# Fused attention and two expert layers on one core: q tiles loaded ahead, half of the pack products moved into the first unit, another scratch order

## The chip, the cores and the metric

One core of a Trainium2 chip (trn2). The metric is the device time of one execution in microseconds, lower is better. The engines are TensorE (PE; its weight loads are PEld), VectorE (DVE), ScalarE (ACT), GpSimd (POOL) and SyncE (SP), whose queue issues nearly all transfers of the kernel before.

## The reference, cut to what matters

```python
def _attn_ref(q, k, v, p):                  # q, k, v: 8 x 8 x 576 x 64; p: 8 x 8 x 32 x 64
    p_packed = sm_attn(p, k, v)             # 32 packs per head attend to 576 keys
    return sm_attn(q, p_packed, p_packed)   # 576 queries attend to the 32 packs
# x = that, as 4608 tokens x 512
h = np.maximum(x @ w_in, 0.0)               # 512 x 2048
x = h * h @ w_out                           # 2048 x 512
# then one of 8 experts (512 -> 1024 -> 512) for each token, by the argmax of its gate
```

`sm_attn` is a softmax attention with scale 1/8. The inputs are float32, but `w_in` and `w_out` arrive as float64.

## The kernel before, in words

The output of the second attention is never built. For each batch the packed heads are multiplied with `w_in` once, head by head: pw has 256 rows (8 heads x 32 packs) and 2048 columns for a batch, and the softmax weights of the second attention (256 for a token) times pw are the hidden layer.

**Opening.** `with tc.manual_schedule()` (L901) writes the order out by hand. A loop over i = 0 .. 18 (L914) runs a pipeline over 16 quads (a batch and half of its heads): `scores(i)` on PE, `greatest` and `normalise` on VectorE and ScalarE, `turn_a(i - 2)` and `values(i - 3)` on PE, and `packs(i - 3)` (L356), which copies the packed heads into `pp33`. Beside it `load_k`, `load_v` and `load_in` issue transfers on SyncE, a slab of `w_in` is converted from float64 (`conv_in`, four VectorE operations and one on ScalarE), and from i = 10 a step of `att2(0)` (L429) is taken: the second attention of the first 384 tokens, in three tiles of 128, of three steps each. A tile's first step issues the load of its q tile (L436, tile `qT`, two buffers) and then the scores against `pp33` (L440). So the loads of the three q tiles are issued at i = 10, 13 and 16.

From i = 11 `pw_quad` (L366), called a pack product here, is taken: for four batches, a pair of heads and a block of 512 columns two 64-row products on PE (j = 0, 1), a copy from PSUM into a staging tile `pws` (L388 on ScalarE or L390 on VectorE, two buffers), and a store of 512 KB on SyncE to the scratch `pw_d` (L391). There are 16 for batches 0 to 3 and 16 for 4 to 7. Five are in i = 11 .. 15, then two, three and four, then ten in a loop (L958) among four `conv_out` (the slabs of `w_out`) and the first `split_pw`; the last eight come in the first unit, in `others` (L975), where the two copies are one on each engine (L385, L386). `load_pw` (L406) brings a block of pw back (batch, 512 columns) in four transfers of 128 KB; it needs the four stores of that block. `split_pw` (L413) cuts it into two parts of reduced precision on ScalarE and GpSimd.

**Main loop.** Twelve units of 384 tokens (L1017); for each of 16 row blocks f of the hidden layer `layer1` (L475) multiplies pw with the softmax weights (L486, or L492 to L495 where a unit lies in two batches), squares, and `layer2` (L508) accumulates with `w_out` (L512). `att2` of the next unit, the gate of the unit before and the routing run beside it. The two expert layers follow (L802, L824).

Every engine, SyncE too, takes its instructions in the program's order; behind the opening a scheduler in the framework sets that order when the kernel is built, and may put the first unit's instructions between those of the opening's end. Eight slots count the transfers in flight: each transfer waits, on the engine that issues it, for the one eight places before it in the program.

## Time and profile before

| what | value |
|---|---|
| three runs, median (lowest to highest) | 1317.05 us (1314.45 to 1319.13) |
| the profiled execution | 1315.94 us, span 1314.0 us |
| PE busy | 1227.0 us, 93% of the span |
| DVE, ACT, POOL busy | 62%, 47%, 21% |
| mean granted TensorE clock | 0.967 |
| the chain that ended last | PE 69%, DVE 13%, DMA 10% |

Times in the profile are microseconds from the span's start. A busy share is an average over the stages, so the stages are read one by one.

### The profile page before, as it was taken

The page shows a single profiled execution, that of the slowest core. Times are in us where ns is not written, and L with a number is a line of the kernel's source. Part 1 is how long each engine was busy: PE and PEld are TensorE (multiplying, and loading weights), DVE is VectorE, ACT ScalarE, POOL GpSimd, SP SyncE. Part 2 cuts the span into 40 slices and gives each one's busy share as a digit, 9 for nine tenths or more (in the row PEclk, how much of TensorE's full clock was granted, in tenths as well). Part 3 has the DMA queues.
Part 4 walks back from the last instruction along what each step waited for, and adds up shares of the span by engine and source line. Part 5 has one row for each costly group of instructions (what it writes and reads, how often), then busy time and mean ns, then how long its engine had stood idle before and what let it go on. Part 6 is the DMA issues. An engine that isn't in the chain of part 4 may idle for free.

```text
span 1314.0 us, 17851 instructions
## 1 busy us (share of the span) xinstructions
PE 1227.0 (93%) x6036; PEld 989.3 (75%) x6036; DVE 815.0 (62%) x2141; ACT 617.4 (47%) x1292; POOL 281.4 (21%) x353
## 2 busy tenths in 40 slices
PE   7578579999999999999999999989999999999995
PEld 5455146888888888888888887877788888888884
DVE  7546477396874976569587578877843543354341
ACT  5334444667545665546755466641432432343230
POOL 4000444433200222102221023100320220132011
PEclk9879669999999999999999999999999999999998
DMA  9956876122201222102220112231532542453310
GB/s 349 352 195 202 271 234 214 57 73 57 66 17 44 83 63 65 33 25 65 75 72 25 49 33 85 88 137 57 194 107 86 194 145 84 159 176 104 106 65 34
DMA packets 76853, 149.22 MB, mean 114 GB/s; under 512 B 7248, under 2 KB 26832, under 8 KB 76624
## 3 DMA queue, kind: packets, MB, share of 16 engines
q1 hardware_dynamic: 70992, 128.81, 29.6%
q0 software_dynamic: 5760, 19.17, 4.6%
q8 instruction: 49, 0.80, 0.3%
q14 instruction: 52, 0.43, 0.1%
HBM read 112.01 MB, written 35.95 MB: 113 GB/s over the span
## 4 chain that ended last, share of the span: by engine, by line
PE 69%; DVE 13%; DMA 10%; issue 3%; ACT 2%; POOL 1%; SPq 1%; POOLq 0%; DVEq 0%; ACTq 0%
PE acc L512 22%; PE h L802 15%; PE o L824 15%; PE ph L486 9%; DVE rows L533 5%; DMA pw_d<-pws 3%; PE s L440 2%; DMA wraw<-in_moe_w 1%; DMA rows<-in_k 1%; DMA qT<-in_q 1%; DVE r L499 1%; DMA wgb<-in_k 1%; DVE ghl L505 1%; PE tr L782 1%; PE pq L354 1%
## 5 line engine op out<-in xcount | busy, mean ns | idle before, releaser
L512 PE MATMUL acc<-wb,ghl 128*128 128x512 f32 x1728 | 444.8, 400 | 3.8 <-ACT ghl L503 3.6
L512 PEld LDWEIGHTS acc<-wb,ghl 128*128 128x128 f32 x1728 | 319.7, 189 | 71.7 <-ACT ghl L503 8.9
L533 DVE SCALAR_TENSOR_TENSOR rows<-rows,wgb 128x512 f32<-128x512 f32 x288 | 213.4, 741 | 3.7
L802 PE MATMUL h<-xt,wb 128*128 128x512 f32 x864 | 214.9, 399 | 0.7 <-DVE ht L813 0.7
L802 PEld LDWEIGHTS h<-xt,wb 128*128 128x128 f32 x864 | 162.8, 189 | 40.6 <-DVE ht L813 1.7
L505 DVE TENSOR_TENSOR ghl<-r,ghl 128x384 fp32r<-128x384 f32 x176 | 103.7, 590 | 80.4 <-ACT ghl L503 80.0
L503 ACT ACTIVATE ghl<-r 128x384 fp32r<-128x384 f32 x192 | 100.2, 522 | 101.2 <-PE acc L512 99.3
L813 DVE SCALAR_TENSOR_TENSOR ht<-h,ht 128x512 fp32r<-128x512 f32 x72 | 49.2, 688 | 115.9 <-ACT ht L812 115.7
L824 PE MATMUL o<-head,ht 128*128 128x512 f32 x432 | 113.3, 396 | 3.8 <-ACT ht L812 3.4
L824 PE MATMUL o<-ring,ht 128*128 128x512 f32 x432 | 112.5, 395 | 0.0
L812 ACT ACTIVATE ht<-h 128x512 fp32r<-128x512 f32 x72 | 42.5, 593 | 144.8 <-PE h L802 144.7
L835 POOL DMA_INDIRECT out<-wgb,idx_s x36 | 36.7, 1019 | 344.8 <-DVE wgb L833 254.0
L502 ACT ACTIVATE r<-r 128x384 f32<-128x384 f32 x192 | 100.2, 523 | 4.6
L824 PEld LDWEIGHTS o<-head,ht 128*128 128x128 f32 x432 | 80.1, 188 | 23.3 <-ACT ht L812 4.5
L417 POOL TENSOR_TENSOR ring<-praw,ring 128x256 fp32r<-128x256 f32 x70 | 59.2, 850 | 177.9 <-ACT ring L416 169.7
L824 PEld LDWEIGHTS o<-ring,ht 128*128 128x128 f32 x432 | 80.1, 188 | 16.8
L486 PE MATMUL ph<-a2T,ring 128*128 128x384 f32 x420 | 86.0, 341 | 0.0
L501 ACT ACTIVATE r<-ph 128x384 f32<-128x384 f32 x128 | 61.6, 482 | 44.7 <-PE ph L486 36.6
L486 PEld LDWEIGHTS ph<-a2T,ring 128*128 128x128 f32 x420 | 74.3, 188 | 5.0 <-issue 0.9
L417 POOL TENSOR_TENSOR head<-praw,head 128x256 fp32r<-128x256 f32 x58 | 48.6, 841 | 133.8 <-ACT head L416 123.8
L460 POOL TENSOR_TENSOR e<-e,sm 128x256 f32<-128x256 f32 x36 | 27.2, 757 | 228.3 <-DVE sm L459 188.8
L486 PE MATMUL ph<-a2T,head 128*128 128x384 f32 x348 | 74.4, 347 | 1.8 <-DVE pws L390 1.4
(198 smaller groups left out, 1707.8 us busy)
## 6 DMA issues: line engine op xcount, KB each, us to landing
wraw<-in_moe_w SPq DMA_DIRECT2D x72, 512.0 KB, 3.8
pw_d<-pws SPq DMA_DIRECT2D x32, 512.0 KB, 4.1
praw<-pw_d SPq DMA_DIRECT2D x128, 128.0 KB, 2.9
x_d<-rows SPq DMA_DIRECT2D x12, 792.0 KB, 3.9
qT<-in_q SPq DMA_DIRECT2D x36, 256.0 KB, 2.9
early<-in_v SPq DMA_DIRECT2D x16, 512.0 KB, 8.9
stage<-in_moe_w_in SPq DMA_DIRECT2D x16, 512.0 KB, 8.9
rows<-in_k SPq DMA_DIRECT2D x10, 576.0 KB, 8.6
```

The source lines that it names most:

```text
L417: nc.gpsimd.tensor_tensor(out=t[:, 1], in0=raw, in1=t[:, 0].bitcast(F32), op=ALU.subtract)
L486: nc.tensor.matmul(ph, t[:, x, c, :], a[:, y, c, :], start=(i == 0), stop=(i == 3 * NPC - 1))
L501: nc.scalar.activation(out=r, in_=ph if len(ps) == 1 else r, func=AF.Relu)
L502: nc.scalar.activation(out=r, in_=r, func=AF.Square)
L503: nc.scalar.activation(out=hl[:, 0], in_=r, func=AF.Copy)
L505: eng.tensor_tensor(out=hl[:, 1], in0=r, in1=hl[:, 0].bitcast(F32), op=ALU.subtract)
L512: nc.tensor.matmul(acc[t], hl[:, x, t * P : (t + 1) * P], w_out_block(f)[:, y, :], start=(f == 0 and x == 0 and y == 0), stop=(f == NF - 1 ...
L533: nc.vector.scalar_tensor_tensor(out=junk, in0=row[:, t, :DM], scalar=1.0, in1=wgb[:, e], op0=ALU.mult, op1=ALU.mult, accum_out=one)
L802: nc.tensor.matmul(ph, half1(g, c)[:, x, f * P : (f + 1) * P], xs[c][:, y, :], start=(i == 0), stop=(i == 3 * NDC - 1),)
L812: nc.scalar.activation(out=h[:, 0, :], in_=ph, func=AF.Relu)
L813: nc.vector.scalar_tensor_tensor(out=h[:, 1, :], in0=ph, scalar=0.0, in1=h[:, 0, :].bitcast(F32), op0=ALU.max, op1=ALU.subtract)
L824: nc.tensor.matmul(po, hs[f][:, x, t * P : (t + 1) * P], second(f)[:, y, :], start=(i == 0), stop=(i == 3 * NFE - 1),)
```

## The change

1. The q tiles of the first unit: the first two are loaded at i = 6 and 7, the third behind the first tile's scores (`load_q`, `qts`).
2. `packs` writes the packed heads twice: `pp32`, with zeros beside them, for the scores of the second attention, now with the 64 columns side by side where they were four apart, and `ppq`, without zeros, for the pack products. The second is a copy on ScalarE.
3. Three, four and four pack products in i = 16, 17 and 18, none behind; the other 16 in the first unit, one at an even f and two at an odd one. Three staging tiles for two. Two of the four `conv_out` behind the loop move into the first unit.
4. Stores of products that ScalarE copies are issued by ScalarE; those of VectorE, and all of the first unit, by SyncE.
5. The scratch is ordered by batch, pack and head, so a block of pw comes back in one transfer of 512 KB. Its rows now go by pack and head, so the softmax tile `e` is stored that way and its operations go over it with a step of eight words.
6. To make room: one square tile for two, and the third raw tile of `w_out` is a part of `rows`.

```diff
-    pp33 = pp_p.tile([P, HP, B // 4, 2 * NPK, 4], F32, name="pp32")
+    pp32 = pp_p.tile([P, B, HP, 2 * NPK], F32, name="pp32")
+    ppq = pw_p.tile([P, HP, B, NPK], F32, name="ppq")
-    squares = [pw_p.tile([P, 512], F32, tag="sq", name="sq", bufs=2) for _ in range(2)]
+    squares = [pw_p.tile([P, 512], F32, tag="sq", name="sq") for _ in range(1)]
...
-    pw_d = tc.dram_tile([B // 4, H, P, DFF], F32, name="pw_d")
+    pw_d = tc.dram_tile([B, NPK, H, DFF], F32, name="pw_d")
...
-    RAWS_OUT = [wgf[:, :1024], wgf[:, 1024:2048], xraw]
+    RAWS_OUT = [wgf[:, :1024], wgf[:, 1024:2048], rows[:, :1024]]
...
         for j in range(2):
-            nc.vector.tensor_copy(
-                pp33[j * D : (j + 1) * D, 2 * qd : 2 * qd + 2, b // 4, j * NPK : (j + 1) * NPK, b % 4],
-                pq[j * D : (j + 1) * D, : 2 * own].rearrange("p (g x) -> p g x", g=2)[:, :, j * NPK : (j + 1) * NPK],
-            )
+            js, ns, gs = slice(j * D, (j + 1) * D), slice(j * NPK, (j + 1) * NPK), slice(2 * qd, 2 * qd + 2)
+            src = pq[js, : 2 * own].rearrange("p (g x) -> p g x", g=2)[:, :, ns]
+            nc.vector.tensor_copy(pp32[js, b, gs, ns], src)
+            nc.scalar.activation(out=ppq[js, gs, b, :], in_=src, func=AF.Copy)
...
-                pp33[js, hp, bq, j * NPK : (j + 1) * NPK].rearrange("p n b -> p (n b)"),
+                ppq[js, hp, 4 * bq : 4 * bq + 4].rearrange("p b n -> p (b n)"),
...
-        so = pw_p.tile([P, 2, 512], F32, tag="w5", name="pws", bufs=2)
+        so = pw_p.tile([P, 2, 512], F32, tag="w5", name="pws", bufs=3)
...
-        nc.sync.dma_start(
-            pw_d[bq].rearrange("(g j) r f -> g r j f", j=2)[hp][:, :, fb * 512 : (fb + 1) * 512], so
-        )
+        (nc.scalar if eng == "ACT" else nc.sync).dma_start(dst, so)
...
-        src = pw_d[b // 4].rearrange("(c h) r f -> h r c f", c=NPC)
-        for h in range(H // NPC):
-            nc.sync.dma_start(raw[h * NPK : (h + 1) * NPK], src[h, b % 4 :: 4, :, fb * 512 : (fb + 1) * 512])
+        nc.sync.dma_start(raw, pw_d[b].rearrange("(c n) h f -> (n h) c f", c=NPC)[:, :, fb * 512 : (fb + 1) * 512])
...
+    def load_q(t0):
+        qT = held["at"].tile([P, HP, P], F32, tag="qT", name="qT", bufs=2)
+        nc.sync.dma_start(qT, qT_d[:, t0 : t0 + P].rearrange("(g p) t -> p g t", p=P))
+        return qT
...
+            qT = load_q(t0) if t0 not in qts else qts.pop(t0)
...
-                        pp33[:, g, b // 4, :, b % 4],
+                        pp32[:, b, g, :],
...
+            if u == 0 and r + 2 < UT:
+                qts[t0 + 2 * P] = load_q(t0 + 2 * P)
...
-            e = held["at"].tile([P, H, NPK], F32, tag="e", name="e", bufs=1)
+            et = held["at"].tile([P, NPK, H], F32, tag="e", name="e", bufs=1)
+            e = et.rearrange("p n h -> p h n")
...
-            ef = e.rearrange("p h n -> p (h n)")
+            ef = et.rearrange("p n h -> p (n h)")
...
+            if i in (6, 7):
+                qts[(i - 6) * P] = load_q((i - 6) * P)
             if i >= 10:
                 next(bg)
-            for _ in range({16: 2, 17: 3, 18: 4}.get(i, 1 if i >= 11 else 0)):
+            for _ in range({16: 3, 17: 4, 18: 4}.get(i, 1 if i >= 11 else 0)):
                 pw_quad(0, made, "ACT" if i < 16 or made % 2 else "DVE")
...
-        for w in range(10):
-            bq, pu = divmod(made, NU)
-            pw_quad(bq, pu, "ACT" if made % 2 else "DVE")
-            made += 1
-            if w % 3 == 0:
-                for _ in conv_out(2 + w // 3):
-                    pass
-            if w in (2, 4, 6):
-                split_pw(0, w // 2)
+        for w in (2, 3):
+            split_pw(0, w - 1)
+            for _ in conv_out(w):
+                pass
+        split_pw(0, 3)
...
-        if made < 2 * NU:
-            pw_quad(1, made - NU, None)
-            made += 1
-        if f + 6 < NU:
-            for _ in conv_out(f + 6):
+        for _ in range(1 + f % 2):
+            if made < 2 * NU:
+                pw_quad(1, made - NU, None)
+                made += 1
+        if f + 4 < NU:
+            for _ in conv_out(f + 4):
```

The order that this gives on the engines, at three places. SyncE, the first q tile, before (the rows are i = 9's last transfers, the tile, and the next k tile behind it; `rows` and `wgb` hold k tiles, `stage` slabs of `w_in`, `early` v tiles):

```order
L242 DMA stage<-in_moe_w_in 128x1024
L281 DMA early<-in_v 128x1024
L284 DMA early<-in_v 64x256
L436 DMA qT<-in_q 128x4x128
L272 DMA rows<-in_k 128x2x576
```

And with the change, from i = 6 on:

```order
L281 DMA early<-in_v 128x1024
L284 DMA early<-in_v 64x256
L431 DMA qT<-in_q 128x4x128
L272 DMA rows<-in_k 128x2x576
L242 DMA stage<-in_moe_w_in 128x1024
L281 DMA early<-in_v 128x1024
L284 DMA early<-in_v 64x256
L431 DMA qT<-in_q 128x4x128
L272 DMA rows<-in_k 128x2x576
```

The tile moves ahead of four k tiles, their slabs and their v tiles; a second one follows an iteration later.

SyncE again, at the end of the opening, where blocks of pw are stored (from `pws`) and brought back (to `praw`, the first of these block 0 of batch 0, then block 1, then 2). Before:

```order
L391 DMA pw_d_135<-pws_902 128x2x512
L391 DMA pw_d_135<-pws_908 128x2x512
L410 DMA praw_911<-pw_d_135 32x2x512 x4
L391 DMA pw_d_135<-pws_952 128x2x512
L391 DMA pw_d_135<-pws_958 128x2x512
L391 DMA pw_d_135<-pws_964 128x2x512
L410 DMA praw_967<-pw_d_135 32x2x512 x4
L246 DMA wgb_84<-in_moe_w_out 128x1024
L391 DMA pw_d_135<-pws_1003 128x2x512
L391 DMA pw_d_135<-pws_1009 128x2x512
L410 DMA praw_1142<-pw_d_135 32x2x512 x2
L391 DMA pw_d_135<-pws_1015 128x2x512
```

With the change (`pws_935` is product 6, 984 and 996 are 8 and 10, 1040 and 1052 are 12 and 14, all counted from 0):

```order
L431 DMA qT_1390<-in_q 128x4x128
L393 DMA pw_d_134<-pws_935 128x2x512
L408 DMA praw_944<-pw_d_134 128x2x512
L393 DMA pw_d_134<-pws_984 128x2x512
L393 DMA pw_d_134<-pws_996 128x2x512
L408 DMA praw_1005<-pw_d_134 128x2x512
L246 DMA wgb_84<-in_moe_w_out 128x1024
L408 DMA praw_1102<-pw_d_134 128x2x512
L393 DMA pw_d_134<-pws_1040 128x2x512
L393 DMA pw_d_134<-pws_1052 128x2x512
```

The odd products' stores are gone from this queue, and block 2 is now asked for before the stores of products 12 and 14.

PE, inside the first unit (`pw` pack products, `ph` layer 1, `acc` layer 2), before:

```order
L512 MATMUL acc<-wb_1043,ghl 128x512 x3
L376 MATMUL pw<-wi_116,pp_85 128x512
L486 MATMUL ph<-a2T,head 128x384 x2
L376 MATMUL pw<-wi_116,pp_85 128x512
L486 MATMUL ph<-a2T,head 128x384 x6
L512 MATMUL acc<-wb_1100,ghl 128x512 x9
L376 MATMUL pw<-wi_116,pp_85 128x512 x2
```

And with the change:

```order
L493 MATMUL ph<-a2T,head 128x384 x8
L519 MATMUL acc<-wb_1076,ghl 128x512 x7
L376 MATMUL pw<-wi_113,ppq 128x512
L519 MATMUL acc<-wb_1076,ghl 128x512 x2
L474 MATMUL ta_1294<-ident,e 128x128 x2
L376 MATMUL pw<-wi_113,ppq 128x512
L493 MATMUL ph<-a2T,head 128x384 x9
L519 MATMUL acc<-wb_1130,ghl 128x512 x9
L376 MATMUL pw<-wi_113,ppq 128x512
L519 MATMUL acc<-wb_1130,ghl 128x512 x4
L376 MATMUL pw<-wi_113,ppq 128x512 x2
```

A row without a count is one 64-row product alone; `x2` is two that follow each other. The whole first unit holds ten alone and three pairs before, and 21 alone, four pairs and a run of three with the change.

## Rows read from the trace of the kernel before

**Rows 1.** The page's busy tenths in 40 slices, PE and its clock

```profile
PE   7578579999999999999999999989999999999995
PEclk9879669999999999999999999999999999999998
```

**Rows 2.** Windows: stretch, length, busy PE, PEld, DVE, ACT, POOL; clock, DMA share, GB/s

```profile
0.00:54.00 54.00, 41.30 (x293) 30.42 (x293) 40.76 (x104) 28.58 (x53) 17.97 (x47) 1.00 0.99 359
54.00:104.00 50.00, 30.49 (x173) 20.92 (x175) 19.66 (x52) 15.11 (x27) 2.32 (x3) 0.73 0.63 216
104.00:174.10 70.10, 44.89 (x191) 21.00 (x190) 37.48 (x64) 27.36 (x51) 21.52 (x25) 0.74 0.77 250
174.10:258.10 84.00, 80.30 (x336) 56.69 (x337) 47.73 (x77) 45.29 (x95) 37.68 (x33) 0.94 0.47 156
258.10:1314.00 1055.90, 1030.04 (x5047) 860.27 (x5046) 669.38 (x1846) 501.04 (x1068) 201.88 (x245) 0.99 0.26 84
```

**Rows 3.** Timeline of PE, 54 to 115 us: start, length, instructions, idle time before

```profile
66.02 1.94 PE L440 MATMUL s<-pp,qT 128*128 128x64 f32 x8 [13.72 <-DMA qT<-in_q]
...
82.51 2.50 PE L354 MATMUL pq<-atbuf,early 128*128 128x128 f32 x20
...
92.50 1.94 PE L440 MATMUL s<-pp,qT 128*128 128x64 f32 x8 [7.49 <-DMA qT<-in_q]
...
103.94 1.19 PE L307 MATMUL s<-wgb,ptb 128*64 128x288 f32 x8
...
114.78 1.15 PE L440 MATMUL s<-pp,qT 128*128 128x64 f32 x8 [3.02 <-DMA qT<-in_q]
```

**Rows 4.** Timeline of SyncE's queue (SPq), the first q tile's issue

```profile
57.66 0.39 SPq L436 DMA_DIRECT2D qT<-in_q  x1
```

**Rows 5.** Groups by line: count, busy us, mean ns, idle before: the copies

```profile
L388 ACT ACTIVATE pws<-pw 128x1024 f32<-128x1024 f32 x15 | 15.3, 1018 | 37.4 <-PE pw L376 19.2 <-DMA pw_d<-pws 16.1 <-issue 2.2
...
L390 DVE COPY pws<-pw 128x1024 f32<-128x1024 f32 x9 | 11.0, 1221 | 18.4 <-DMA pw_d<-pws 14.2 <-PE pw L376 4.2
...
L361 DVE COPY pp<-pq 64x64 f32<-64x64 f32 x32 | 8.7, 272 | 5.6 <-PE pq L354 5.2
```

**Rows 6.** Timeline of PE, 174 to 258 us, the first unit

```profile
174.12 2.29 PE L486 MATMUL ph<-a2T,head 128*128 128x384 f32 x6 [1.37 <-DVE pws L390]
...
196.50 1.12 PE L376 MATMUL pw<-wi,pp 64*128 64x512 f32 x2
...
219.51 1.13 PE L376 MATMUL pw<-wi,pp 64*128 64x512 f32 x4
...
220.56 2.35 PE L512 MATMUL acc<-wb,ghl 128*128 128x512 f32 x9
...
255.98 2.35 PE L512 MATMUL acc<-wb,ghl 128*128 128x512 f32 x9
```

**Rows 7.** Page, DMA issues: engine, count, size, us to landing

```profile
pw_d<-pws SPq DMA_DIRECT2D x32, 512.0 KB, 4.1
```

**Rows 8.** Waits, 104 to 174.1 us: total, times, longest

```profile
PE pw L376 <- ACT pws L388: 15.7, 8, 4.6
...
DVE pws L390 <- DMA pw_d<-pws: 14.2, 3, 7.0
```

**Rows 9.** Windows of 20 us, inside the first unit

```profile
200.00:220.00 20.00, 19.48 (x83) 12.19 (x83) 19.72 (x28) 11.55 (x23) 10.01 (x9) 1.00 0.46 153
```

**Rows 10.** Groups by line: the softmax of the second attention

```profile
L451 DVE TENSOR_TENSOR e<-s,mx 128x256 f32<-128x256 f32 x36 | 15.1, 419 | 1.5
...
L457 DVE TENSOR_REDUCE sm<-e 128x8 f32<-128x256 f32 x36 | 14.9, 414 | 5.4 <-ACT e L455 5.1
...
L455 ACT ACTIVATE e<-e 128x256 f32<-128x256 f32 x36 | 14.8, 410 | 10.4 <-DVE e L451 10.2
...
L460 POOL TENSOR_TENSOR e<-e,sm 128x256 f32<-128x256 f32 x36 | 27.2, 757 | 228.3 <-DVE sm L459 188.8 <-PE tb L339 25.9 <-DMA qT<-in_q 5.1
```

**Rows 11.** Waits of PE, 174.1 to 258.1 us

```profile
PE pw L376 <- ACT pws L385: 1.6, 1, 1.6
```

More of the change, by code (lines that the diff above doesn't have):

```diff
@@ L93, in tile_pack_attention_moe_moe2 @@
     wgb = wg_p.tile([P, NE, DM], F32, name="wgb")
-    pp33 = pp_p.tile([P, HP, B // 4, 2 * NPK, 4], F32, name="pp32")
-    nc.gpsimd.memset(pp33, 0.0)
-    squares = [pw_p.tile([P, 512], F32, tag="sq", name="sq", bufs=2) for _ in range(2)]
+    pp32 = pp_p.tile([P, B, HP, 2 * NPK], F32, name="pp32")
+    nc.gpsimd.memset(pp32, 0.0)
+    ppq = pw_p.tile([P, HP, B, NPK], F32, name="ppq")
+    squares = [pw_p.tile([P, 512], F32, tag="sq", name="sq") for _ in range(1)]
     whole = [pw_p.tile([P, 512], F32, tag="tf", name="tf", bufs=2) for _ in range(2)]
-    xraw = pw_p.tile([P, 1024], F32, name="xraw")
     lg_all = const.tile([P, NTL, NE], F32, name="lg_all")
@@ L248, in conv_in @@
     def conv_in(u):
-        raw, m = words(RAWS_IN[u % 4]), squares[u % 2]
+        raw, m = words(RAWS_IN[u % 4]), squares[0]
         square(m, raw)
@@ L253, in conv_out @@
     def conv_out(u):
-        raw, m, tf = words(RAWS_OUT[u % 3]), squares[u % 2], whole[u % 2]
+        raw, m, tf = words(RAWS_OUT[u % 3]), squares[0], whole[u % 2]
         square(m, raw)
@@ L382, in pw_quad @@
             )
-        so = pw_p.tile([P, 2, 512], F32, tag="w5", name="pws", bufs=2)
+        so = pw_p.tile([P, 2, 512], F32, tag="w5", name="pws", bufs=3)
+        dst = pw_d[4 * bq : 4 * bq + 4].rearrange("b n h f -> (b n) h f")
+        dst = dst[:, 2 * hp : 2 * hp + 2, fb * 512 : (fb + 1) * 512]
         if both is None:
@@ L427, in parts @@
         return got
+    qts = {}
+    def load_q(t0):
+        qT = held["at"].tile([P, HP, P], F32, tag="qT", name="qT", bufs=2)
+        nc.sync.dma_start(qT, qT_d[:, t0 : t0 + P].rearrange("(g p) t -> p g t", p=P))
+        return qT
     def att2(u):
@@ L434, in att2 @@
             c0 = r * P
-            qT = held["at"].tile([P, HP, P], F32, tag="qT", name="qT", bufs=2)
-            nc.sync.dma_start(qT, qT_d[:, t0 : t0 + P].rearrange("(g p) t -> p g t", p=P))
+            qT = load_q(t0) if t0 not in qts else qts.pop(t0)
             s2 = bank("t", "s2")
```

## The prediction

> **What bounds the kernel now.** I read the busy slices first [rows 1]: TensorE (PE) is full from about slice 7 to the end, and only the first sixth has gaps and a lowered clock. Cut into stages [rows 2], the 1055.9 us from 258.1 on hold 1030.0 us of PE work at a clock of 0.99: nothing outside TensorE can give much there. The time to be had lies in three stretches. From 54 to 104 us PE is busy 30.5 of 50 us at 0.73 of its clock; from 104 to 174.1 it is busy 44.9 of 70.1 at 0.74; from 174.1 to 258.1, the first unit of the main loop, 80.3 of 84 at 0.94. So the sum goes by three marks on PE's timeline: the last scores product of the opening (103.94 [rows 3]), the first layer-1 product (174.12) and the first unit's last accumulation (starts 255.98, ends about 258.1) [rows 6]. Whatever moves the third mark moves the end by as much, if the later units stay as they are.
>
> **Stage 1, up to the last scores.** Before 103.94 PE waits twice for q tiles, 13.72 and 7.49 us, and once later for 3.02 [rows 3]. The tile is asked for at 57.66 [rows 4], when PE has already run dry, and the transfers stand at a share of 0.99 [rows 2], so it lands some 8 us later. After each of the two the clock is still low: the same eight instructions that take 1.15 us the third time take 1.94 [rows 3], and the mean of the stretch is 0.73 [rows 2]. With the products that follow I put this at 2.5 us each time, three times what the eight lose. Without waits: 103.94 - 21.2 - 5 = 77.7. Against it: two tiles of 0.26 MB now lie earlier in a saturated stream of 359 GB/s [rows 2], 2 x 0.73 = 1.5 us; and every `packs` gets two more ScalarE copies, which the program makes take turns with VectorE's two. Such a copy is 0.27 us [rows 5]; the turn-taking can hold VectorE 0 to 1 us in each of 13 iterations. Nearest is the low end, because in the saturated iterations both engines wait for loads anyway: 1 us in all. That gives 80.5, a gain of 23. The stream is a floor of its own: all that must land before the last scores is some 27.9 MB (16 k tiles, 14 v, 15 w_in, q, p, two stores); 19.4 MB are in by 54 us, the rest at 359 GB/s takes 23.7, so about 78. Bounds of the gain: 15 and 26.
>
> **Stage 2, last scores to first layer-1.** It takes 174.1 - 103.9 = 70.2 us now. In it PE waits for the copies that empty its banks (15.7 us in 8 waits) and the copies for the stores that empty theirs (14.2 us in 3 on VectorE alone) [rows 8]: with two staging tiles a product is through only when a store of 4.1 us [rows 7] has landed. Twenty pack products go by in this time: one in iteration 15, nine in 16 to 18, ten in the loop behind. Now eleven are left after iteration 15 and three tiles carry them. A tile's round is a copy of 1.02 or 1.22 [rows 5], about 0.4 for the issue, the store of 4.1: 5.6 us for three products. From scores(15) to the first of the eleven PE needs what it needs now without the wait, (115.9 - 103.9) - 3.0 = 9 us. Products 1 to 3 find free tiles, and the other eight take three rounds less a little: 17 us, plus the first copy and queue, 2. The last of the sixteen would be copied at 80.5 + 9 + 19 = 108.5. Then I add what the order of SyncE's queue costs: the load of the third block of pw stands ahead of the stores of products 12 and 14 (counted from 0) and itself waits until the second block is loaded (3.9 at most) and split on GpSimd; I take 6 us. ScalarE then still splits the third block (4 x 0.4) and copies the last product before it turns to the first block's own split: 3 us. The first layer-1 product so starts at 117.5, 37 us after the scores: a gain of 33. The eight products and the two w_out conversions that go into the unit are what makes the difference; the stores on ScalarE's queue I cost at nothing by themselves, because ScalarE in its turn waits 0.4 us per issue. Bounds: 20 if SyncE's chain holds twice as long, 40 if it costs nothing.
>
> **Stage 3, the first unit.** Now 84.0 us. It gets eight more products and two more conversions. PE's price is not the 1.05 us of a pair: two 64-row products that follow each other run together (four instructions in 1.13 us, the next starting 1.05 behind them), one alone takes the same (two instructions in 1.12) [rows 6]. Counted in the order above, the unit now has ten single products and three pairs, 13 places; with the change 21 singles, four pairs and a run of three, 27 places. 14 x 1.05 = 14.7 us, all on PE, which is the bound here. Beside it I take 3 us of new waits: the fourth block's load goes out only when the last products are stored, and ScalarE stands behind it before it empties the second layer-1 bank. Longest wait of a product on a copy now: 4.6 [rows 8]; two of these are the other end, so 0 to 9. VectorE: it is full today from 200 to 220 [rows 9] but busy only 47.7 of 84 us [rows 2], with ten conversions in them, so no more than 4.8 us each; two more, and eight copies of half of 1.22 us [rows 5], make it 62 at most in a unit of over 100. No charge. Sum: 84 + 17.7 = 101.7, a loss of 18 (15 to 28).
>
> **The later units.** The contiguous score operand changes nothing: eight instructions of 64 columns take 1.15 us and twenty of 128 columns, already contiguous, 2.50 [rows 3], 0.14 against 0.125 each, so the columns do not set the pace. One load of 512 KB for four of 128 saves SyncE 96 issues that nobody waits for. What may cost is the turned softmax tile: four operations a tile now touch words 32 bytes apart. No row shows such a step; today they are 0.42 and 0.41 us on VectorE, 0.41 on ScalarE, 0.76 on GpSimd [rows 10]. From below: nothing, since the tile is made a whole unit ahead. From above: all of them twice as long, with VectorE's share of 1.6 us a unit pushed onto the evictions that PE waits for, 11 units, 18 us. I take 0, since PE is busy 1030 of 1056 us there and VectorE 669 [rows 2].
> Here the Trainium skill speaks against the change: SBUF — State Buffer, section "Door 1: The DMA port swizzle", says that accesses which each fall on a new 16-byte line pay a penalty, with four fp32 as the free step, and GPSIMD Engine Reference, section "7. Performance pitfalls for Q7 kernels", gives 2.9 for 1.9 cycles an element when GpSimd reads with a step of over 8 bytes. No run here shows it; by that ratio GpSimd's multiply would become an estimated 1.15 us, and the sum would stay as it is unless the delay reaches PE, which is the first rival.
>
> **Sum.** -23 - 33 + 18 = -38 us. The profiled execution took 1315.94 (span 1314.0), so 1278; the median of the three runs is 1317.05, 1.1 above it. Forecast: **1278 us**. Worst ends together: -15 - 20 + 28 = -7; best: -26 - 40 + 15 = -51.
>
> **Rivals.**
> *The strided softmax reaches PE.* For it: VectorE has stretches at the start of each unit where it hardly rests. Against: PE stands idle only 26 of the 1055.9 us there, for whatever cause [rows 2]. Price up to 18: 1278 + 18 = **1296**. Chance 0.08. (The two pages of the Trainium skill that are named above are its case.)
> *The gate moves instead of opening.* SyncE executes in order, and the block loads wait for stores, splits and each other. If the first layer-1 starts at 135, not 117.5, the gain of stage 2 is 15.5: **1295**. For it: the waits on stores in [rows 8]. Against: eight fewer stores stand in that queue. Chance 0.12.
> *The stores saturate stage 1.* Each of iterations 11 to 15 moves 1.7 MB of loads and 0.52 MB of store; ScalarE, which must wait for a free transfer slot before it issues, then holds up the softmax behind it. Scores(15) at 90: **1288**. Chance 0.10.
> *Slower: products in the unit stop PE.* PE takes them in order between layer-1 and layer-2 products, and each needs a bank that ScalarE and VectorE empty into a staging tile that a store must free. 16 products have to hold PE 38/16 = 2.4 us each beyond the above for the gain to be gone; at the longest wait of today, 4.6 us [rows 8], it is 16 x 4.6 = 74 on top: 1278 + 74 = **1352**. Against: in this unit today PE waits for a copy once, 1.6 us [rows 11]. Chance 0.04.
> *More than I think.* The stream delivers as now, SyncE's chain costs nothing: -50, **1266**. Chance 0.14.
> The forecast's own case, 1269 to 1288, has 0.52.
>
> **How the numbers follow.** A measurement of this kernel tells 0.3%, 4 us, from no change. All cases but the fourth lie well below 1313; of the worst ends (-7) only a sliver falls within 0.3%. Faster 0.94, same 0.02, slower 0.04. The range takes in the own case, the first three rivals and most of the good one: 1264 to 1298.
>
> **What would show it.** Right: no q wait on PE before the last scores, which start near 80; the first layer-1 product near 117; 101 us from there to the end of the first unit's accumulations, with the clock near 1 after its first 20 us; PE work after that as now, 1056 us. Wrong: scores(15) at 90 or later with transfers at share 1 (stage 1); a first layer-1 after 125 with SyncE waiting for splits (stage 2); PE waits on ScalarE's or VectorE's bank copies of over 10 us in the unit (stage 3); a last stretch of more than 1060 us, with longer softmax operations (strides).

## Result, and the profile after

With the change the median of four runs is **1283.41 us** (1278.41 to 1284.8) against 1315.75 of the kernel before in the same rounds: a ratio of 0.9746, 95% interval 0.971 to 0.9782. The forecast was 1278, with 1264 to 1298 as its range. The profiled execution took 1284.8, its span is 1282.9.

The page of the changed kernel, PE and its clock in 40 slices, answers to [rows 1]:

```profile
PE   6886799999999999999999998999999999999995
...
PEclk8998899999999999999999999999999999999998
```

The clock, 0.6 in slices 5 and 6 before, stays at 0.8 or more, and PE is full one slice sooner. The windows of the changed kernel, cut at its own marks, answer to [rows 2] (columns as there; the stretches are the loads, up to the last scores, up to the first layer-1 product, the first unit, the rest):

```profile
0.00:54.00 54.00, 40.80 (x289) 31.00 (x290) 35.92 (x96) 29.48 (x63) 18.18 (x47) 0.94 1.00 349
54.00:82.60 28.60, 24.86 (x177) 17.43 (x176) 20.50 (x53) 16.67 (x36) 2.44 (x3) 1.00 1.04 380
82.60:126.10 43.50, 29.20 (x165) 17.15 (x165) 27.55 (x55) 22.61 (x45) 9.32 (x11) 0.92 0.77 267
126.10:228.00 101.90, 92.68 (x356) 57.20 (x357) 67.56 (x95) 55.88 (x114) 53.45 (x47) 0.95 0.58 191
228.00:1282.90 1054.90, 1026.46 (x5054) 859.49 (x5052) 684.15 (x1848) 513.00 (x1074) 210.32 (x246) 0.99 0.25 84
```

The stretch behind 54 us is 28.6 long where it was 50, at full clock, with the transfers at a share of 1.04: the stream of loads is full now. The next is 43.5 where it was 70.1. The first unit is 101.9 where it was 84.0. What follows is 1054.9 where it was 1055.9.

PE's timeline of the changed kernel (columns as in [rows 3]) has the marks and the q tiles:

```profile
54.49 1.00 PE L444 MATMUL s<-pp,qT 128*128 128x64 f32 x8
...
73.52 1.00 PE L444 MATMUL s<-pp,qT 128*128 128x64 f32 x8
...
82.64 1.19 PE L307 MATMUL s<-wgb,ptb 128*64 128x288 f32 x8 [1.05 <-ACT abuf L319]
...
93.76 1.00 PE L444 MATMUL s<-pp,qT 128*128 128x64 f32 x8
...
117.94 5.39 PE L376 MATMUL pw<-wi,ppq 64*128 64x512 f32 x14 [7.13 <-DVE pws L392]
126.10 0.62 PE L493 MATMUL ph<-a2T,head 128*128 128x384 f32 x2 [2.77 <-ACT head L414]
...
135.88 1.65 PE L519 MATMUL acc<-wb,ghl 128*128 128x512 f32 x6 [1.11 <-ACT ghl L510]
...
144.07 2.92 PE L519 MATMUL acc<-wb,ghl 128*128 128x512 f32 x6 [3.96 <-ACT ghl L510]
...
227.44 0.85 PE L519 MATMUL acc<-wb,ghl 128*128 128x512 f32 x3
```

The three products of q tiles (L444) wait for nothing; in [rows 3] they waited 13.72, 7.49 and 3.02 us, and the first two took 1.94 where these take 1.00. The last scores start at 82.64 (103.94 before), the first layer-1 product at 126.10 (174.12), and the 144 accumulations of the first unit end at about 228 (258.1), with the row at 227.44. PE waited 7.13 us for a bank at 117.94 and 2.77 for a split at 126.10, and in the first unit 1.11 and 3.96 us for the layer-2 operand.

All runs by the same marks of their profiles (us; "behind it" is the span less the unit's end), and the median of each run's executions. The unit's end is read off merged rows and lies up to 0.6 us before the end of the last product, so smaller differences in the two columns that use it say nothing. The rows below the second are the experiments of the next section:

| run | last scores | first layer-1 | unit's end | behind it | median |
|---|---|---|---|---|---|
| before | 103.9 | 174.1 | 258.1 | 1055.9 | 1315.8 |
| the change | 82.6 | 126.1 | 228.0 | 1054.9 | 1283.4 |
| q tiles as before (e1_q_late) | 106.3 | 145.0 | 241.2 | 1051.7 | 1295.6 |
| before, q ahead alone (e2_q_alone) | 78.1 | 148.3 | 231.8 | 1049.1 | 1281.5 |
| flat softmax (e3_softmax_flat) | 81.4 | 125.6 | 225.3 | 1045.7 | 1275.8 |
| stores on SyncE (e4_stores_sync) | 78.7 | 121.0 | 222.1 | 1052.6 | 1274.8 |
| order of the splits (e5_gate) | 83.0 | 116.9 | 212.8 | 1052.9 | 1268.7 |
| four loads (e6_four_loads) | 83.0 | 127.7 | 227.5 | 1052.6 | 1281.5 |
| paired products (e7_pairs) | 81.9 | 126.9 | 232.4 | 1051.8 | 1286.7 |
| products as before (e8_products_early) | 82.4 | 153.8 | 238.0 | 1057.5 | 1301.3 |
| two staging tiles (e11_two_tiles) | 82.9 | 130.2 | 225.6 | 1052.5 | 1280.8 |
| e3, e4 and e5 together (e9_best) | 79.0 | 113.9 | 213.2 | 1045.1 | 1260.2 |
| e4 and e5 (e10_gate_sync) | 80.8 | 117.0 | 214.2 | 1051.6 | 1267.4 |
| e9 and e7 (e12_best_pairs) | 79.9 | 114.5 | 214.3 | 1043.0 | 1263.4 |

### The profile page after: what moved, and what is told of

It is laid out like the page before. It is cut to its first block, busy times and chain, and to the rows that moved or that the text cites. A ratio compares the mean times of both kernels' runs of the same rounds, so it can differ in the third digit from the quotient of the medians.

```text
span 1282.9 us, 17702 instructions
## 1 busy us (share of the span) xinstructions
PE 1214.0 (95%) x6036; PEld 982.3 (77%) x6036; DVE 835.7 (65%) x2145; ACT 637.6 (50%) x1328; POOL 293.7 (23%) x353
## 4 chain that ended last, share of the span: by engine, by line
PE 71%; DVE 15%; DMA 6%; ACT 3%; issue 3%; POOL 2%; ACTq 0%; POOLq 0%; SPq 0%; DVEq 0%
PE acc L519 23%; PE h L809 15%; PE o L831 15%; PE ph L493 9%; DVE rows L540 5%; PE pw L376 2%; DMA wraw<-in_moe_w 2%; PE s L444 2%; DVE r L506 1%; PE tr L789 1%; DVE ghl L512 1%; DMA wgb<-in_k 1%; DMA pw_d<-pws 1%; PE pq L354 1%; DMA early<-in_v 1%
## 5 line engine op out<-in xcount | busy, mean ns | idle before, releaser
L512 DVE TENSOR_TENSOR ghl<-r,ghl 128x384 fp32r<-128x384 f32 x176 | 106.5, 606 | 72.6 <-ACT ghl L510 72.3
L831 PEld LDWEIGHTS o<-head,ht 128*128 128x128 f32 x432 | 80.6, 189 | 23.7 <-ACT ht L819 5.0
L415 POOL TENSOR_TENSOR ring<-praw,ring 128x256 fp32r<-128x256 f32 x70 | 62.1, 892 | 155.8 <-ACT ring L414 150.3
L467 POOL TENSOR_TENSOR e<-e,sm 128x256 f32<-128x256 f32 x36 | 36.0, 1000 | 228.3 <-DVE sm L466 158.9
L415 POOL TENSOR_TENSOR head<-praw,head 128x256 fp32r<-128x256 f32 x58 | 51.4, 888 | 105.0 <-ACT head L414 105.0
```

Of the source, the lines that this page charges most:

```text
L415: nc.gpsimd.tensor_tensor(out=t[:, 1], in0=raw, in1=t[:, 0].bitcast(F32), op=ALU.subtract)
L512: eng.tensor_tensor(out=hl[:, 1], in0=r, in1=hl[:, 0].bitcast(F32), op=ALU.subtract)
L831: nc.tensor.matmul(po, hs[f][:, x, t * P : (t + 1) * P], second(f)[:, y, :], start=(i == 0), stop=(i == 3 * NFE - 1),)
```

## The experiments

**q tiles.** The first edit takes the q loads of the changed kernel back to the step that uses them:

```diff
-            if u == 0 and r + 2 < UT:
-                qts[t0 + 2 * P] = load_q(t0 + 2 * P)
...
-            if i in (6, 7):
-                qts[(i - 6) * P] = load_q((i - 6) * P)
```

> The changed kernel with one part undone: each q tile of the first unit is again asked for in the step that uses it. Its marks with the change: last scores at 82.64, first layer-1 product at 126.10, end of the first unit's accumulations 228.3, span 1282.9. My theory (the wait for q sets stage 1): PE waits 12 to 15 us for the first tile and 5 to 10 for the second again, the last scores start near 102, the first layer-1 near 146, and the time is 1283 + 20 = 1303 (1297 to 1308). Rival A (another part of the change, such as fewer bytes ahead or the stores on the other queue, shortened stage 1): last scores within 5 us of 83, time 1283 to 1288. Rival B (what follows has slack): last scores near 102, but first layer-1 before 136, time below 1294.

The two waits came back:

```profile
67.67 1.94 PE L444 MATMUL s<-pp,qT 128*128 128x64 f32 x8 [14.19 <-DMA qT<-in_q]
...
95.96 1.94 PE L444 MATMUL s<-pp,qT 128*128 128x64 f32 x8 [9.55 <-DMA qT<-in_q]
```

The last scores moved to 106.3, 23.7 later. But the time is 1295.6 (ratio to before 0.9859, 0.984 to 0.9878), only 12 above the change and just under the theory's range: the stretch behind the scores was 4.8 shorter, the unit 5.7 and the rest 3.2. So the theory holds for the stage, and part of rival B for what follows. One reason shows in this run's trace: ahead of the split that opens layer 1 ScalarE waits 0.49 us for a later block, where with the change it waits 3.60 and 4.85 (under "Order of the splits"). What else there is in the 13.7, no run tells.

The second edit gives the kernel before those loads, and nothing else: `load_q` and the two places above.

> The kernel before with one part of the change alone: the first two q tiles asked for at i = 6 and 7, the third behind the first tile's scores. Marks before: last scores 103.94, first layer-1 174.12, end of the first unit 258.1. My theory (the stages add up): last scores near 83, then the 70 us of stage 2 and the 84 of the first unit as before, so first layer-1 near 153 and 1316 - 21 = 1295 (1291 to 1300). Rival (the stores and the loads of pw behind the opening run at a pace of their own, which the q waits only hid): first layer-1 later than 162, 1304 to 1316.

It took 1281.5 (0.9742, 0.9725 to 0.9758), as fast as the whole change. PE's timeline of this run:

```profile
70.02 1.09 PE L446 MATMUL s<-pp,qT 128*128 128x64 f32 x8
...
78.10 1.19 PE L307 MATMUL s<-wgb,ptb 128*64 128x288 f32 x8
...
148.34 1.97 PE L494 MATMUL ph<-a2T,head 128*128 128x384 f32 x5 [1.36 <-DVE pws L390]
```

The last scores start at 78.10, 25.8 sooner; from there to layer 1 it is 70.2 and the unit 83.5, as before to half a microsecond. So the two stretches behind the scores kept their length, as the theory has it. It missed 4.9 us in the last scores (83 expected) and the 6.8 us behind the unit (1049.1 for 1055.9); the build places later instructions anew after every edit, and no run tells whether that is all of these 6.8.

**Products.** This edit puts the products and conversions of the changed kernel back where they stood (two, three and four, then ten in the loop, eight in the unit).

> The changed kernel with pack products and conversions where they stood before (two, three and four in i = 16 to 18, ten in the loop behind, eight in the first unit); q ahead, three staging tiles, stores on two queues and the new scratch order stay. My theory (a product moved costs as much on PE in the unit as it saves ahead): first layer-1 near 142, the unit near 88, time 1284 (1278 to 1290). Rival A (with three tiles the opening takes a product cheaper than the unit does): first layer-1 below 136, time 1270 to 1277. Rival B (behind the opening the stores still set the pace, 2.7 us or more a product): first layer-1 at 148 or later, 1291 or more.

Rival B came: first layer-1 at 153.8, time 1301.3 (0.9901, 0.9876 to 0.9926). The stretch behind the scores is 71.4 with three staging tiles and two queues, as long as the 70.2 with two tiles and one. It is the eight products moved, with their two conversions, that are worth 27.9 us there, not the third tile; the unit grows by 17.7 for them. No run moves the conversions alone. The waits of PE and the copies in this stretch, first of this run, then of the change (columns as in [rows 8]):

```profile
PE pw L376 <- ACT pws L390: 16.7, 4, 5.1
...
PE pw L376 <- DVE pws L392: 6.9, 3, 5.9
```

```profile
PE pw L376 <- DVE pws L392: 7.1, 1, 7.1
...
ACT pws L390 <- DMA pw_d<-pws: 4.4, 2, 3.7
```

PE waits 16.7 + 6.9 us for copies with twenty products, 7.1 (and 1.4 in a smaller row) with twelve.

The tiles by themselves: `bufs=3` of `pws` to `bufs=2` in the changed kernel.

> The changed kernel with two staging tiles for the stores of the pack products in place of three. My theory (a tile's round of copy, issue and landing, 5.6 us, sets the pace of the eleven products that come after the loop's fifteenth pass): eight of them take four rounds of two in place of three less a little, so the first layer-1 product comes 4 to 8 us later, at 130 to 134, and the unit with its sixteen products a little later too, time 1288 to 1293. Rival (the order in which ScalarE takes splits, packs and products sets it, whatever the number of tiles): first layer-1 within 2 us of 126.1, time 1280 to 1286.

The first layer-1 product came 4.1 us later, in the expected range, but the unit was 95.4 for 101.9 and the time 1280.8 (0.9727, 0.9692 to 0.9763), no different from the change and below the 1288 to 1293 of the theory. What starts later there waits less: PE stands idle 4.8 of those 95.4 us, 9.2 of the 101.9; the other 2 us are of its own work.

**Order of the splits.** ScalarE's timeline of the changed kernel at the end of the opening (`head` and `ring` from `praw` are splits, `ppq` the packs, `pws` the product copies):

```profile
113.94 1.33 ACT L414 ACTIVATE head<-praw 128x256 fp32r<-128x256 f32 x4 [3.60 <-DMA praw<-pw_d]
115.18 0.20 ACT L364 ACTIVATE ppq<-pq 64x64 f32<-64x64 f32 x1
...
116.20 1.02 ACT L390 ACTIVATE pws<-pw 128x1024 f32<-128x1024 f32 x1
...
122.07 1.34 ACT L414 ACTIVATE ring<-praw 128x256 fp32r<-128x256 f32 x4 [4.85 <-DMA praw<-pw_d]
124.16 1.02 ACT L390 ACTIVATE pws<-pw 128x1024 f32<-128x1024 f32 x1 [0.75 <-DMA pw_d<-pws]
...
125.63 0.42 ACT L414 ACTIVATE head<-praw 128x256 fp32r<-128x256 f32 x1 [0.44 <-ACT pws L390]
```

The four splits at 113.94 are block 1's, those at 122.07 block 2's, the one at 125.63 block 0's first: the build has put later blocks ahead. ScalarE waits 3.60 us for block 1 with the last packs ready behind it (VectorE waits 6.45 for them, PE 7.13 for VectorE's product copy behind that), and 4.85 for block 2 with the split that opens layer 1 behind it. The edit fixes the order by hand:

```diff
+            if i == NQ + 2:
+                for f in range(4):
+                    split_pw(0, f)
...
-            if i in (16, 17):
-                load_pw(0, i - 16)
-        split_pw(0, 0)
+            if i == 16:
+                load_pw(0, 0)
+            if i == NQ + 2:
+                load_pw(0, 1)
...
-            split_pw(0, w - 1)
...
-        split_pw(0, 3)
...
+        load_pw(0, 2)
+        for f in range(4, 12):
+            split_pw(0, f)
...
-        if f + 4 < NF:
+        if 12 <= f + 4 < NF:
```

> The changed kernel with the first three blocks of pw in another order by hand: block 0 is split right behind the last packs, block 1 is loaded behind the last stores of the opening, and the splits of blocks 1 and 2 stand behind the last conversions. With the change ScalarE waited 3.6 us for block 1 and 4.9 for block 2 before it came to the last packs, the last product and block 0's own split; PE waited 7.1 us behind that for a bank and 2.8 for the split. My theory (that order is what the first layer-1 product, at 126.1, waits for): it starts at 113 to 116, the waits for blocks 1 and 2 are gone from ScalarE ahead of it, and the time is 1273 (1269 to 1277). Rival A (the first unit is then held by the slabs of w_out, which arrive when they do): first layer-1 at 113 to 116, but the unit over 110 us long, time 1280 to 1285. Rival B (the products wait for free staging tiles in any order): first layer-1 at 121 or later, time 1279 to 1285.

ScalarE and PE in this run:

```profile
111.19 1.32 ACT L414 ACTIVATE head<-praw 128x256 fp32r<-128x256 f32 x4
112.41 1.01 ACT L390 ACTIVATE pws<-pw 128x1024 f32<-128x1024 f32 x1
...
115.85 1.02 ACT L390 ACTIVATE pws<-pw 128x1024 f32<-128x1024 f32 x1 [2.42 <-DMA pw_d<-pws]
```

```profile
112.93 1.99 PE L376 MATMUL pw<-wi,ppq 64*128 64x512 f32 x8 [1.80 <-DVE pws L392]
116.92 1.51 PE L493 MATMUL ph<-a2T,head 128*128 128x384 f32 x6 [2.00 <-ACT pws L390]
```

The splits of block 0 wait for nothing, and of the two product copies shown one waits, 2.42 us for a store. First layer-1 at 116.9 (113 to 116 expected), 34.0 behind the scores in place of 43.5, and the unit is not longer but 6 us shorter, 95.9: its layer-2 operands are no longer late. Time 1268.7 (0.9648, 0.9628 to 0.9668), 4 better than expected, for that reason.

**Stores.** In the changed kernel every store on SyncE: `(nc.scalar if eng == "ACT" else nc.sync).dma_start(dst, so)` becomes `nc.sync.dma_start(dst, so)`.

> The changed kernel with all stores of pack products issued by SyncE. Marks with the change: last scores 82.64, first layer-1 126.10, end of the first unit 228.0, span 1282.9. My theory (who issues the store matters little, since the three staging tiles and the landing of the stores set the pace): all marks within 4 us, time 1278 to 1289. Rival A (SyncE takes its queue in order, so stores stand behind loads of pw that wait, and these behind stores): first layer-1 132 or later, 1289 to 1300. Rival B (ScalarE lost time by issuing): first layer-1 120 to 123, 1276 to 1279.

1274.8 (0.9689, 0.9664 to 0.9714): 8.6 faster than the change, beyond even rival B. The last scores come 4.0 sooner. ScalarE's timeline of the changed kernel shows the price (ACTq is its queue of transfers):

```profile
64.40 1.02 ACT L390 ACTIVATE pws<-pw 128x1024 f32<-128x1024 f32 x1
67.50 0.40 ACTq L393 DMA_DIRECT2D pw_d<-pws  x1
...
76.83 1.02 ACT L390 ACTIVATE pws<-pw 128x1024 f32<-128x1024 f32 x1
80.86 0.37 ACTq L393 DMA_DIRECT2D pw_d<-pws  x1
```

The copy ends at 65.42 and its store goes out at 67.50; the next copy shown ends at 77.85, its store goes out at 80.86. ScalarE's next work, `atbuf`, which PE's values need, stands behind each. The order has every such store wait for a slot, so for the transfer eight places before it, and the stream is full there. The trace has these landings: the slab of `w_in` that SyncE issued at 58.11 lands at 67.42, its v tile of 69.82 at 80.78, and each store goes out 0.08 us behind. With all stores on SyncE, `atbuf` follows its copy at once:

```profile
73.83 1.02 ACT L390 ACTIVATE pws<-pw 128x1024 f32<-128x1024 f32 x1
74.75 0.59 ACT L344 ACTIVATE atbuf<-ta 128x512 f32<-128x512 f32 x1
```

With the order of the splits set by hand as well (e10_gate_sync, below) the last scores come 2.2 sooner, layer 1 no sooner at all (117.0 for 116.9), and the time is 1.2 lower: the two edits save the same time.

The Trainium skill, DMA: Bandwidth & Descriptors, section "Issuing engines are not separate DMA queues", says that issuing from several engines saves only the time of the issue. The rows agree that an issue is short, 0.37 to 0.40 us here, and add that issuing can cost more than that: the wait in front of it is up to 3.0.

**Softmax tile and loads.** With the change the tile is "turned", stored by pack and head. Here it is stored by head again ("flat"), and a block of pw comes back in four loads, one for each of four heads; then the changed kernel with four loads of the same rows, which takes the loads by themselves:

```diff
-            et = held["at"].tile([P, NPK, H], F32, tag="e", name="e", bufs=1)
-            e = et.rearrange("p n h -> p h n")
+            e = held["at"].tile([P, H, NPK], F32, tag="e", name="e", bufs=1)
...
```

> The changed kernel with the softmax tile stored by head again, so its four operations go over neighbouring words; a block of pw then comes back in four loads of 128 KB, one for each of four heads. My theory (later units are PE's, and the longer softmax operations, 0.66 for 0.42 us on VectorE twice, 0.74 for 0.41 on ScalarE, 0.97 for 0.62 on GpSimd, lie beside it): the operations fall back to their old length, the stretch behind the first unit stays within 4 us of 1054.6, and the time is 1279 to 1288. Rival A (the longer operations reach PE): 36 tiles with 0.48 us less on VectorE give back up to 17 us, time 1266 to 1275. Rival B (four loads for one hold up SyncE's queue at the end of the opening): first layer-1 3 to 8 us later, time 1287 to 1292.

> The changed kernel with each block of pw brought back in four loads of 128 KB in place of one of 512 KB; rows and softmax tile as with the change. The flat softmax tile, which came with four loads, stood at 1275.8. My theory (the flat tile gave the 8 us, not the loads): within 4 us of the changed kernel, 1279 to 1288, and 1055 behind the first unit. Rival (four loads on more of the time gave it): 1272 to 1278.

The groups of the softmax and the scores by line, first of the change, then of the flat tile (columns as in [rows 10]):

```profile
L467 POOL TENSOR_TENSOR e<-e,sm 128x256 f32<-128x256 f32 x36 | 36.0, 1000 | 228.3 <-DVE sm L466 158.9 <-ACT ghl L510 26.7 <-PE ph L493 15.9
...
L462 ACT ACTIVATE e<-e 128x256 f32<-128x256 f32 x36 | 26.3, 731 | 16.1 <-DVE e L458 11.6 <-DVE sm L553 2.8 <-DVE mx_all L547 1.3
...
L458 DVE TENSOR_TENSOR e<-s,mx 128x256 f32<-128x256 f32 x36 | 23.8, 660 | 1.0
...
L464 DVE TENSOR_REDUCE sm<-e 128x8 f32<-128x256 f32 x36 | 23.5, 654 | 14.6 <-ACT e L462 14.3
...
L444 PE MATMUL s<-pp,qT 128*128 128x64 f32 (+1 forms) x320 | 39.1, 259 | 0.0
```

```profile
L468 POOL TENSOR_TENSOR e<-e,sm 128x256 f32<-128x256 f32 x36 | 29.5, 819 | 223.0 <-DVE sm L467 174.7 <-ACT pws L390 35.7 <-ACT r L510 5.3
...
L463 ACT ACTIVATE e<-e 128x256 f32<-128x256 f32 x36 | 14.9, 413 | 12.3 <-DVE e L459 12.0
...
L459 DVE TENSOR_TENSOR e<-s,mx 128x256 f32<-128x256 f32 x36 | 15.1, 419 | 0.9
L465 DVE TENSOR_REDUCE sm<-e 128x8 f32<-128x256 f32 x36 | 15.0, 416 | 7.6 <-ACT e L463 7.3
```

A step of eight words takes VectorE's operations from 0.42 to 0.66 us, ScalarE's from 0.41 to 0.73, GpSimd's from 0.82 (0.76 before the change) to 1.00. The flat tile is 1275.8 (0.9708, 0.9681 to 0.9735); the four loads alone are 1281.5 (0.9738, 0.9712 to 0.9763), no different from the change. So the tile costs 5.7 us between these two, whose intervals overlap, and 7.3 between the two runs below with and without it (1267.4 and 1260.2), whose intervals do not. The flat tile's time lies between the ranges of the theory and of rival A: rival A's mechanism is there, its price under half of the 17. How it reaches PE shows in the windows from the unit's end to the first product of the expert layers, with four loads and the turned tile, then flat:

```profile
228.10:838.90 610.80, 601.29 (x3158) 517.86 (x3156) 474.25 (x1468) 376.51 (x862) 137.10 (x154) 1.00 0.19 60
...
225.40:826.60 601.20, 596.73 (x3153) 515.69 (x3153) 459.86 (x1457) 367.78 (x862) 126.58 (x154) 1.00 0.19 60
```

PE is idle 9.5 us (610.80 less 601.29) against 4.5: 5.5 against 2.1 of it in small waits for the layer operands that VectorE and ScalarE make, 2.6 against 1.0 for a transfer of the expert layers. Its own busy time is 4.6 longer, for which no row gives a reason.

**Pairs.** In the first unit the two 64-row products get one tile of two banks, so that they follow each other; the other uses of the three banks share the one that is left.

> The changed kernel; in the first unit the two 64-row products of a pack product get one PSUM tile of two banks, so that they must follow each other, and the other uses of the three banks one bank until the unit is over. My theory (a lone 64-row product costs PE as much as a pair, 1.05 us): 27 places become 16 or 17, the unit falls from 101.9 to 90.5 (88 to 94), and the time is 1272 (1268 to 1276). Rival A (with one tile the products wait for their copies): PE waits for the copies more than 8 us in the unit, which stays above 96; 1278 to 1285. Rival B (the unit goes at the pace at which w_out is converted): unit 97 or more with PE waiting for layer-2 operands, 1278 to 1285.

Rival A, by its waits and its unit: 1286.7 (0.9792, 0.9759 to 0.9824), no faster than the change, the unit 105.6. PE's products by line in the first unit, first before, then of the change, then with pairs:

```profile
L376 PE MATMUL pw<-wi,pp 64*128 64x512 f32 x32 | 17.2, 731 | 2.0 <-ACT pws L385 1.6 <-DVE a2T L471 0.4
```

```profile
L376 PE MATMUL pw<-wi,ppq 64*128 64x512 f32 x58 | 29.8, 704 | 2.2 <-ACT pws L387 1.2 <-DVE pws L388 0.9
```

```profile
L379 PE MATMUL pw<-wi,ppq 64*128 64x512 f32 x60 | 21.7, 807 | 8.2 <-DVE pws L391 8.2
...
DVE pws L391 <- ACT pws L390: 25.2, 9, 4.2
```

The products' time on PE falls from 29.8 to 21.7 us, but the two copies that empty the one tile now take turns (VectorE waits 25.2 us for ScalarE's), and PE waits 8.2 for them.

**Together.** The order of the splits, the flat tile and the stores on SyncE; the same without the flat tile; and with the pairs.

> Three edits of the changed kernel at once: the hand-set order of the first three blocks (alone 1268.7), the flat softmax tile with four loads (alone 1275.8) and all stores on SyncE (alone 1274.8), each against 1283.4. My theory (three separate places: the gate at the end of the opening, the later units, ScalarE's wait for a transfer slot in the opening): the gains add, 14.7 + 7.6 + 8.6 = 31, time 1252 (1248 to 1258), last scores near 79, first layer-1 near 110, behind the first unit about 1045. Rival A (the gate and the stores save the same wait of ScalarE): the two give 15 to 18 together, time 1258 to 1262. Rival B (the stores on SyncE stand in front of the loads of w_out that the unit then lacks): the first unit over 100 us, time 1260 or more.

> As the run before without the flat softmax tile: the softmax tile by pack and head and one load a block, as with the change. A second pair with and without it, in another order of the later instructions. My theory (the turned tile costs some 8 us by itself): 7 to 10 us more than the run before, 1260, and 608 to 612 us from the first unit's end to the first product of the expert layers, where flat tiles give about 601. Rival (most of the 8 us of the first pair came from the order that the build happened to give): within 4 us of the run before.

> The three edits together (1260.2) and the paired products of the first unit. With the change alone the pairs saved 11 places on PE, 29.8 us of products falling to 21.7, but PE waited 20.5 us in the unit for other engines, 8.2 of it for the products' copies, 5 for the first block's split, 2.7 for w_out, 2.4 for a bank, and its clock fell to 0.89. My theory (with the split early and ScalarE free of stores, the copies come in time): the unit falls from 99.8 to 88 to 95 us, time 1249 to 1256. Rival (one tile of two banks makes each product wait for both copies, wherever the splits stand): PE waits 8 us or more for the copies, the unit stays at 98 or more, 1259 to 1266.

1260.2 (0.9565, 0.9539 to 0.959), 1267.4 (0.9621, 0.9597 to 0.9645) and 1263.4 (0.961, 0.9594 to 0.9626). The first is the fastest version, 23 us ahead of the change. It missed the sum of 1252 by 8, as rival A has it: the order and the stores together give 16.0, not 23.3. The turned tile costs its 7.3 a second time. The pairs give nothing here either, as their rival has it: PE is busy 82.9 of the unit's 99.8 us where it was 96.8 of 99.3 without them, so the 14 us that they take off PE's work come back as waiting, 8.1 of it until 200 us for the copies that take turns.

## Why the prediction was right, point by point

**Stage 1** (a gain of 23 forecast, 21.3 measured) is right by its mechanism: no q wait is left, the clock stays up, and e1 and e2 move the last scores by 23.7 and 25.8 with nothing else. The stream as a floor of 78 is where e2 (78.1) and e4 (78.7) ended; but PE was as full as the stream there (in e2 busy 23.75 of the 24.1 us from 54 on, with transfers at a share of 1.05), so no run tells which of the two sets that mark. The term that failed is what the rest of the change costs here: forecast were 1.5 us for two tiles in the stream and 1 for the packs' turn-taking (their sum gives 80.2, not 80.5), and nothing for the stores on ScalarE's queue. The packs are at most the 0.6 that e4 lies above e2; the stores are the 4.0 between e4 and the change. The rival of the stores had named that wait, with too high a price (scores at 90).

**Stage 2** (a gain of 33 forecast, 26.7 measured; 43.5 us in place of 37). The term of 9 us for the order on SyncE and ScalarE was right in place and size: setting it by hand takes 9.5 off, though the wait is ScalarE's for the loads of two later blocks, and the split that SyncE was to wait for costs it 0.7 us; ahead of the third block's load it waits 7.3 for that block's own stores. The other 28 failed: with the order set by hand they came out at 34.0. From the last scores to the first of the last eleven products "what it needs now without the wait", put at 9 us, is 12 (82.6 to 94.7), in which PE waits 1.75 us for the packs on ScalarE and 1.22 for the longer softmax; with a flat tile and no stores on ScalarE (e9) it is 9.7. And "the other eight take three rounds" fails as a rule for the pace: the third tile is worth 3.9 us of this stage (47.3 with two) and none of the total, and e8's twenty products go no faster with it than the kernel before without. The gain is from products that left. The rival "the gate moves" (the gate is what the first layer-1 product waits for; 135 in the rival) was half true: 126.1, also past the 125 that the prediction had named as its sign of being wrong here.

**Stage 3** (a loss of 18 forecast, 17.9 measured: the unit took 101.9 where 101.7 was forecast). The sum is right by luck, as its two terms are each off by some 2 and to opposite sides: PE's work grew by 12.4 us (92.68 for 80.30) where 14.7 stood, its waits by 5.5 (9.2 for 3.7) where 3 stood. Six of the 64 product instructions ran ahead of the unit (58 in the row under "Pairs"); in e5, with all 64 in it, PE is busy 94.55 us, 14.3 more than before, so the 14.7 was well sized. The waits hang on the gate: in e5 PE waits 1.5 us in this unit. VectorE's "62 at most" failed, 67.56, without being what PE waits for.

**The later units** (nothing forecast, 1.0 of gain measured) are right by luck, as a sum of terms of both signs that the forecast set to nothing, and of what the build's order happens to give (6.8 us in e2). "The contiguous score operand changes nothing" failed: its 320 instructions take 39.1 us, 0.259 on average, where the same group of the kernel before took 47.4 in all with 0.299; between the first unit's end and the expert layers, where the clock was 1.00 in both, it is 36.3 and 32.0, 4.3 us of PE's time, in the same mix of two shapes:

```profile
L440 PE MATMUL s<-pp,qT 128*128 128x64 f32 (+1 forms) x252 | 36.3, 293 | 0.0
...
L444 PE MATMUL s<-pp,qT 128*128 128x64 f32 (+1 forms) x256 | 32.0, 259 | 0.0
```

The operand had its words 16 bytes apart. Of this step the Trainium skill, SBUF — State Buffer, section "Door 1: The DMA port swizzle", can be read both ways: an access that goes to a new 16-byte line pays, and four fp32 are named as the free step. The two rows agree with the first reading. "I take 0" for the strided softmax failed too: it is 5.7 and 7.3 us in two pairs of runs, between the 0 and the 18 of the bounds. (The 18 took 1.6 us of VectorE a unit; by [rows 10] it is 0.83 a tile and three tiles a unit, 2.5, so 27.) PE's small idle share was no cover: with the turned tile it waited six times, 2.6 us in all, for VectorE's layer operand, and twice, 0.5 in all, with the flat one. From the Trainium skill, GPSIMD Engine Reference, section "7. Performance pitfalls for Q7 kernels", came the estimate of 1.15 us for the multiply; it is 1.00, 0.76 before.

**The sum** was -38 and came out at -31 in the profiled executions: of the 7 missing, 1.7 are from stage 1 and 6.3 from stage 2, and the later units gave 1.0 back. No rival decided it; two of them, the gate and the strided tile, each took a part. What the prediction did not see at all is that the loads ahead are the whole gain: e2 alone is 34 us faster than before (25.8 of it up to the last scores, 6.8 behind the unit for no known reason). Against it the changed kernel is 26.7 shorter in stage 2, but 4.5 longer in stage 1, 18.4 in the unit and 5.8 behind it: in these profiled executions the moved products are worth some 10 net in stage 2 and the unit (17.9 on the whole by the medians of e8 and the change), and the stores on ScalarE (8.6) and the turned tile (5.7 to 7.3) give them back.

## What to carry to other kernels

Cut the span at marks that everything passes, and cost a change for each stretch: the stages added up within a few microseconds even where the reasons differed. Where a scheduler orders the engines, read ScalarE's and SyncE's order at the seam between two phases before a load is moved; a split of a later block that waits for its load ahead of the one that opens the next phase cost 9.5 us, and a few lines of hand-set order returned it. Be wary of letting an engine that computes issue transfers while the stream is full (8.6 us here), and do not take an engine's idle share as cover for longer steps in front of a bound engine that needs their result (5.7 to 7.3).

## What was not expected of the hardware

Operations over a tile with 32 bytes between their words took 1.57 times as long on VectorE (0.419 to 0.660 us), 1.78 on ScalarE (0.410 to 0.731) and 1.32 on GpSimd (0.757 to 1.000; 0.819 with the flat tile again), the same 128 x 256 values each. A product whose moving operand had its 64 columns 16 bytes apart took 0.293 us on average in the later units, 0.259 with them side by side, at a clock of 1.00 in both. And an engine that only has to issue a store stood up to 3.0 us in front of it, until a transfer that another engine had issued had landed (80.78 us, the store at 80.86).
